# A transformer block with segmented memory attention and a gated FFN: from two stages to one hand-ordered stream

## The chip, the cores and the metric

The kernel runs on one core of a Trainium2 chip. The metric is device time in microseconds (us) per execution. Five engines work side by side, each with its own queue: TensorE (PE in the profile; its weight loads are PEld), VectorE (DVE), ScalarE (ACT), GpSimd (POOL) and SyncE (SP), which issues most transfers. Before the change three runs took 403.99, 404.45 and 406.45 us; the median is 404.45.

## What is computed

One block over 2048 tokens of 448 features, in bf16. A condition vector `c` gives six modulation rows; the first part is attention with 16 heads of 28 features in 4 segments of 512 tokens, the second a gated FFN with 1792 hidden features.

```python
mod = (_silu(c) @ w_mod).reshape(c.shape[0], 6, 1, -1)        # sa, ca, ga, sb, cb, gb
h = _layernorm(x, axis=-1) * (1 + ca) + sa
x = x + ga * _A_ref(h, A_wq, A_wk, A_wv, A_wo, A_beta)
h = _layernorm(x, axis=-1) * (1 + cb) + sb
x = x + gb * _B_ref(h, B_w_gate, B_w_up, B_w_down)

for s in range(N):                                             # _A_ref, for each segment
    a_dot = softmax(qs @ ks.T * scale + causal_mask) @ vs      # inside the segment
    a_mem = (phi(qs) @ M) / (phi(qs) @ z + 1e-06)              # memory of earlier segments
    outs.append(g * a_mem + (1.0 - g) * a_dot)                 # then @ wo
    M = M + phi(ks).T @ vs;  z = z + phi(ks).sum(over tokens)

h = _sigmoid(x @ w_gate) * (x @ w_up)                          # _B_ref, then @ w_down
```

`phi(t)` is `t + 1` for positive `t` and `exp(t)` otherwise. The memory recurrence `M`, `z` is the only tie between segments. LayerNorm, the `wo` product and the FFN are independent from token to token.

## The kernel before, in words

A scheduler decides, from the dependences and the order of the program, in which order each engine does its work; nothing in this kernel fixes it by hand. The 448 features are cut into chunks of 128, 128, 128 and 64 rows (`_kc_rows`); the last chunk sits in rows 64 to 127, so each product over the features still takes four matmuls.

**Start.** SP loads `x` of segment 0, a third of `w_mod`, then `wq`, `wk` and `wv` in pieces through a tile with three buffers (`wtmp`, L163); VectorE copies each piece into a padded layout with 32 columns a head (L168). GpSimd's queue loads the FFN weights at the same time (L173, L174). The modulation rows are made on one partition (L278), transposed into columns, and folded into the weights: `1 + ca` scales `wq`, `wk`, `wv` (L331 to L333), and `sa` becomes bias columns (`bias_cols`, L306). `prep_b`, called after the second attention unit, does the same for `wg`, `wu`, `wo` and `wd`.

**LayerNorm** (`ln_prep`, `ln_transposes`): mean and variance of four tiles of 128 tokens (L185, L186), a reciprocal root by three Newton steps in tiny VectorE instructions (L188 to L201), the normalised tile `xn` (L205), then TensorE transposes into `h1T` or `h2T` (L215, L216).

**Attention.** A unit is a segment and a group of four heads; there are 16. `unit_logits` makes the transposed logits of four key blocks, of 512, 384, 256 and 128 query columns, with four heads side by side in the array (L388), into one PSUM tile `lg` of four banks with a single buffer; ScalarE takes the exp (L392), VectorE masks the diagonal block with a product (L393). `unit_pv` multiplies with `v` for each query block (L418), adds the memory product (L422), and divides and mixes on VectorE, once per query block (L426 to L440). `flush_o` transposes the result (L403, L404). `seg_end` builds `phi(k)` and updates the memory (L451 to L467). The projections of the next segment (L240 for q and k, L246 for v) are put after the first unit of a segment.

**Joint and FFN.** Only when all 16 units are done are the PSUM pools released and given out anew. For each segment `wo_ln2_prep` makes `x2` (L478, L480, with `x` loaded a second time) and its LayerNorm; `ffn_block` then runs 14 hidden chunks: gate (L512) with tanh on ScalarE (L515), up (L519) with a copy and bias on ScalarE (L522), their product on VectorE (L523), and `down_passes` (L506), which accumulates the four token blocks in four PSUM banks. The sums are added to `x2` and stored (L534, L535) at the end of each segment.

Of the kernel before, what the change touches and what calls it, by code (L numbers as in the profile page):

```python
# [24 lines left out]
def kernel(  # L25
# [18 lines left out]
    assert D == 448  # L44
# [24 lines left out]

    const = ctx.enter_context(tc.tile_pool(name="const", bufs=1))  # L70
# [15 lines left out]
    nc.gpsimd.affine_select(out=ident_bf[:], in_=ident_bf[:], compare_op=ALU.not_equal, fill=1.0,
                            base=0, pattern=[[-1, P]], channel_multiplier=1)
    one11 = const.tile([1, 1], BF16)
    nc.vector.memset(one11[:], 1.0)
    ones1 = const.tile([1, P], BF16)  # L90
    nc.vector.memset(ones1[:], 1.0)
    cols_sb = const.tile([P, 16], F32)
    cols_bf = const.tile([P, 16], BF16)
    g_row = const.tile([P, H], F32)
    omg_row = const.tile([P, H], F32)
    bq_col = const.tile([P, NHC], F32)
    bk_col = const.tile([P, NHC], F32)
    bg_col = const.tile([P, NFC], F32)
    bu_col = const.tile([P, NFC], F32)
    bvrep = const.tile([P, DP], BF16)  # L100
    mask01 = const.tile([P, 4, P], BF16)
    nc.vector.memset(mask01[:], 1.0)
    nc.gpsimd.affine_select(out=mask01[:], in_=mask01[:], compare_op=ALU.is_ge, fill=0.0, base=0,
                            pattern=[[0, 4], [1, P]], channel_multiplier=-1)
    maskcol = const.tile([P, 4], F32)
    nc.vector.memset(maskcol[:], 0.0)
    for hs in range(4):
        nc.vector.memset(maskcol[HP * hs:HP * hs + HP, hs:hs + 1], 1.0)
    M_sb = const.tile([P, NHC, P], F32)
    nc.gpsimd.memset(M_sb[:], 0.0)  # L110
    rhs_mem = const.tile([P, NHC, 4 * MW], BF16)
    nc.gpsimd.memset(rhs_mem[:], 0.0)
    for hs in range(4):
        nc.gpsimd.affine_select(out=rhs_mem[:, :, MW * hs + Dh], in_=rhs_mem[:, :, MW * hs + Dh],
                                compare_op=ALU.not_equal, fill=1e-6, base=-(HP * hs + Dh),
                                pattern=[[0, NHC]], channel_multiplier=1)

    wq_sb = wts.tile([P, NKC, DP], BF16)
    wk_sb = wts.tile([P, NKC, DP], BF16)
    wv_sb = wts.tile([P, NKC, DP], BF16)  # L120
    wo_sb = wts.tile([P, NHC, D], BF16)
    wg_sb = wts.tile([P, NKC, F], BF16)
    wu_sb = wts.tile([P, NKC, F], BF16)
    wd_sb = wts.tile([P, NFC, D], BF16)
    for w_sb in (wq_sb, wk_sb, wv_sb):
        nc.vector.memset(w_sb[:].rearrange("p k (h e) -> p (k h) e", e=HP)[:, :, Dh:HP], 0.0)
        nc.gpsimd.memset(w_sb[0:64, 3, :], 0.0)
# [501 lines left out]
```

## Time and profile before

| | |
|---|---|
| runs (us) | 403.99, 404.45, 406.45; median 404.45 |
| profiled execution | span 402.8 us from first to last instruction; no separate time is listed for it, and the median lies 1.65 us above the span |
| mean granted TensorE clock | 0.821 |
| logits, first and last start (us) | 47.7 and 217.5 |
| first `pwo` matmul / first gate matmul / last `down` matmul (us) | 223.1 / 240.3 / 396.6 |

How to read the lines that follow: a group line gives source line, engine, operation, output and inputs, count, then busy time and mean duration of one in ns, then the engine's idle time just before and what ended it. Lines with a start time, a duration and an instruction are the timeline or the chain of waits, in us. A stretch line gives the start and end, then the busy time of each engine with its number of instructions, the granted clock (1.00 is full speed), the share of the DMA engines and GB/s. PEclk shows the clock in 40 slices, in tenths.

### The profile page before, as it was taken

To read this page: it belongs to the slowest core of one execution; us is meant where nothing else is said; L and a number is where in the kernel's file an instruction comes from. 1 tells how busy PE (TensorE), PEld (TensorE's weight loads), DVE (VectorE), ACT (ScalarE), POOL (GpSimd) and SP (SyncE) were. 2 spreads that over 40 slices of the span, in tenths; PEclk is the share of its full clock that TensorE was granted. 3 is DMA by queue.
4 is the path that set the end of the run, shared out by engine and by line. 5 is a ranking of instruction groups with operands and counts; after the bars stand their busy time and mean duration, and the time that the engine had idled before them with its cause. 6 is when DMAs were issued, how large, how long until landed. Compare 5 with 4: busy or idle time off the path is not lost.

```text
span 402.8 us, 6547 instructions
## 1 busy us (share of the span) xinstructions
PE 316.2 (79%) x2354; PEld 159.4 (40%) x2354; DVE 245.6 (61%) x988; ACT 210.9 (52%) x277; POOL 20.7 (5%) x104
## 2 busy tenths in 40 slices
PE   0407879684789777977766579998999899999993
PEld 0104334242555435344434234543444434444441
DVE  5428995639764988189899677324932385234223
ACT  2103559745756786658765015552565246545551
POOL 9500000000100000000000000000000000000000
PEclk9999959855659555795555669999999989999997
DMA  7993400200000000000000100001100010001001
GB/s 204 283 280 106 132 1 2 62 20 2 3 0 2 2 1 2 0 2 2 2 1 2 46 24 26 0 2 46 46 2 1 24 46 1 2 0 46 2 0 46
DMA packets 11602, 14.76 MB, mean 37 GB/s; under 512 B 1473, under 2 KB 10770, under 8 KB 11570
## 3 DMA queue, kind: packets, MB, share of 16 engines
q1 hardware_dynamic: 10610, 9.53, 8.1%
q0 software_dynamic: 960, 4.82, 3.8%
q8 instruction: 18, 0.29, 0.3%
q14 instruction: 14, 0.11, 0.1%
HBM read 12.51 MB, written 1.84 MB: 36 GB/s over the span
## 4 chain that ended last, share of the span: by engine, by line
PE 55%; DVE 19%; ACT 13%; DMA 9%; issue 3%; SPq 0%; DVEq 0%; POOL 0%; ACTq 0%
PE gps L512 12%; PE ups L519 11%; PE dps L506 10%; ACT pT L392 9%; PE lg L388 4%; DMA wtmp<-in_A_wk_dram 3%; PE lntr L215 3%; PE pq L240 3%; PE pwo L478 2%; PE pk L240 2%; DVE stats L185 2%; DMA wtmp<-in_A_wq_dram 2%; PE pv L246 2%; PE acc L418 2%; DVE ot L534 1%
## 5 line engine op out<-in xcount | busy, mean ns | idle before, releaser
L392 ACT ACTIVATE pT<-lg 128x2048 bf16<-128x2048 f32 (+1 forms) x64 | 79.3, 1239 | 37.3 <-PE lg L388 33.7
L512 PE MATMUL gps<-h2T,wg_sb 128*128 128x512 bf16 x224 | 58.5, 383 | 3.7 <-DVE x L480 3.6
L519 PE MATMUL ups<-h2T,wu_sb 128*128 128x512 bf16 x224 | 58.4, 384 | 0.0
L506 PE MATMUL dps<-wd_sb,hTg 128*128 128x448 bf16 x224 | 51.8, 353 | 1.1 <-DVE hTg L523 0.9
L522 ACT ACTIVATE ub<-ups,bu_col 128x512 bf16<-128x512 f32 x56 | 38.5, 687 | 14.0 <-PE ups L519 14.0
L388 PE MATMUL lg<-qT,kT 32*128 32x512 bf16 (+3 forms) x256 | 31.7, 405 | 15.5 <-ACT pT L392 14.6
L418 PE MATMUL acc<-vt,pT 128*128 128x32 bf16 x640 | 29.3, 187 | 12.2 <-DVE t L437 5.2
L418 PEld LDWEIGHTS <-pT 128*128 128x128 bf16 x640 | 25.6, 104 | 22.3 <-issue 16.9
L393 DVE TENSOR_TENSOR pT<-pT,mask 128x512 bf16<-128x512 bf16 x64 | 26.8, 421 | 11.0 <-ACT pT L392 9.7
L512 PEld LDWEIGHTS <-wg_sb 128*128 128x128 bf16 x224 | 22.1, 99 | 28.4 <-issue 5.8
L519 PEld LDWEIGHTS <-wu_sb 128*128 128x128 bf16 x224 | 22.1, 99 | 27.1 <-issue 1.4
L506 PEld LDWEIGHTS <-hTg 128*128 128x128 bf16 x224 | 21.3, 98 | 26.1 <-DVE hTg L523 4.4
L388 PEld LDWEIGHTS <-kT 32*128 32x128 bf16 x256 | 10.4, 97 | 29.6 <-issue 25.2
L215 PE MATMUL lntr<-ident_bf,xn 128*128 128x128 bf16 x128 | 14.5, 273 | 8.0 <-DVE xn L205 5.7
L240 PE MATMUL pq<-h1T,wq_sb 128*128 128x512 bf16 x64 | 20.3, 433 | 0.0
L240 PE MATMUL pk<-h1T,wk_sb 128*128 128x512 bf16 x64 | 19.2, 403 | 0.0
L216 ACT COPY h1T<-lntr 128x512 bf16<-128x512 bf16 x13 | 7.2, 589 | 21.4 <-PE lntr L215 21.4
L403 PE MATMUL otr<-ident_bf,o_u 128*128 128x128 bf16 x64 | 14.9, 269 | 4.3 <-DVE o_u L438 2.4
L478 PE MATMUL pwo<-wo_sb,oT 128*128 128x448 bf16 x64 | 16.5, 417 | 0.7 <-ACT oT L404 0.7
L248 DVE TENSOR_TENSOR vt<-pv,bvrep 128x512 bf16<-128x512 f32 x16 | 10.9, 688 | 9.0 <-PE pv L246 9.0
L215 PEld LDWEIGHTS <-xn 128*128 128x128 bf16 x128 | 10.6, 120 | 12.7 <-DVE xn L205 6.4
L242 ACT ACTIVATE qT<-pq,bq_col 128x512 bf16<-128x512 f32 x16 | 11.2, 697 | 7.0 <-PE pq L240 7.0
(298 smaller groups left out, 471.3 us busy)
## 6 DMA issues: line engine op xcount, KB each, us to landing
wmod_t<-in_w_mod_dram SPq DMA_DIRECT2D x9, 224.0 KB
x_t<-in_A_x_dram SPq DMA_DIRECT2D x4, 448.0 KB
xr<-in_A_x_dram SPq DMA_DIRECT2D x16, 112.0 KB
out_dram<-ot SPq DMA_DIRECT2D x16, 112.0 KB
wd_sb<-in_B_w_down_dram POOLq DMA_DIRECT2D x1, 1568.0 KB, 17.3
wg_sb<-in_B_w_gate_dram POOLq DMA_DIRECT2D x3, 448.0 KB, 6.1
wu_sb<-in_B_w_up_dram POOLq DMA_DIRECT2D x3, 448.0 KB, 9.9
wo_sb<-in_A_wo_dram SPq DMA_DIRECT2D x16, 24.5 KB
```

The lines of the kernel that those rows point to most:

```text
L215: nc.tensor.transpose(pts[:, t * P:(t + 1) * P], xns[t][:, f0:f0 + P], ident_bf[:])
L240: nc.tensor.matmul(pq[:, 0:L], lhsT=w_sb[:, kc, hc * P:(hc + 1) * P], rhs=h1T[:, kc, :], start=(kc == 0), stop=(kc == NKC - 1))
L388: nc.tensor.matmul(lg4[:, hs, 0:nq], lhsT=kT[HP * hs:HP * hs + 32, hc, q0:q0 + P], rhs=qT[HP * hs:HP * hs + 32, hc, q0:q0 + nq], start=Tru ...
L392: nc.scalar.activation(pT[:, :, ob:ob + nq], lg4[:, :, 0:nq], AF.Exp, scale=scale)
L393: nc.vector.tensor_tensor(pT[:, :, ob:ob + P], pT[:, :, ob:ob + P], mask01[:], ALU.mult)
L403: nc.tensor.transpose(otr[:, qb * P:(qb + 1) * P], o_p[:, qb, :], ident_bf[:])
L418: nc.tensor.matmul(acc[:, hs * 32:(hs + 1) * 32], lhsT=pT[:, hs, c0:c0 + P], rhs=vt[:, kb, h * HP:(h + 1) * HP], start=(kb == 0), stop=(kb ...
L478: nc.tensor.matmul(pw_[:, 0:D], lhsT=oT[:, hc, t * P:(t + 1) * P], rhs=wo_sb[:, hc, :], start=(hc == 0), stop=(hc == NHC - 1))
L506: nc.tensor.matmul(dps[t][:, 0:D], lhsT=hT_fc(fc)[:, t * P:(t + 1) * P], rhs=wd_sb[:, fc, :], start=(fc == 0), stop=(fc == NFC - 1))
L512: nc.tensor.matmul(gps[:, 0:L], lhsT=wg_sb[:, kc, fc * P:(fc + 1) * P], rhs=h2T[:, kc, :], start=(kc == 0), stop=(kc == NKC - 1))
L519: nc.tensor.matmul(ups[:, 0:L], lhsT=wu_sb[:, kc, fc * P:(fc + 1) * P], rhs=h2T[:, kc, :], start=(kc == 0), stop=(kc == NKC - 1))
L522: nc.scalar.activation(ub[:], ups[:, 0:L], AF.Identity, bias=bu_col[:, fc:fc + 1], scale=1.0)
```

## The change

The kernel body is written anew.

- **Chunks.** The features are cut into four chunks of 112 rows. `wv`, `wo`, `o` and `v` are no longer padded to 32 columns a head; `wq` and `wk` are (`q` and `k` keep 32 partitions a head).
- **Modulation.** It no longer touches `wq`, `wk`, `wv`, `wg`, `wu`: the transposed LayerNorm output is multiplied by `1 + ca` and `sa` is added while it is copied out of PSUM (`h_chunk`). The modulation columns come straight from matmuls with `w_mod` as the stationary operand. `wo` and `wd` are still scaled, on GpSimd.
- **Transfers.** Each weight is one or two DMAs; SP's queue holds them in order of use and ScalarE's queue three of them. `wq` and `wk` are staged in the space of `wd`. `x` is loaded once and kept; `x2` replaces it in place. The modulation blocks take turns in two slots.
- **Engines.** Masks, clamps, the LayerNorm root (one `pow`), and the last sum of attention go to GpSimd; the copy of `k` goes to VectorE; gate and up meet in one VectorE instruction that reads PSUM. The division of attention runs once per unit instead of once per query block.
- **Logits** come in three groups a unit: 512 columns, 384 with 128, and 256.
- **Order.** TensorE runs in program order (`manual_schedule`); the other engines are still scheduled. For each segment `s`, a queue `fill` of other work (projections and memory of later segments, `wo`, LayerNorm transposes, gate and up of segment `s-1`, `down` of `s-2`) is cut into 24 portions of equal estimated time and laid between the 12 logits groups, `pv` and `otr`. PSUM is one `lg` tile of four banks and a ring of four banks for all else. `down` runs token block by token block over all 14 hidden chunks.

Cut to its core:

```diff
+    KP, NK = 112, 4
+    OFF = (0, L, 2 * L, 2 * L - P)
+    KB_GROUPS = ((0,), (1, 3), (2,))
...
+    ctx.enter_context(tc.manual_schedule(engines={PE}))
+    ps_lg = ctx.enter_context(tc.tile_pool(name="ps_lg", bufs=1, space=bass.MemoryType.PSUM))
+    ps_m = ctx.enter_context(tc.tile_pool(name="ps_m", bufs=4, space=bass.MemoryType.PSUM))
...
+    load_x(nc.sync, 0, 2)
+    load_x(nc.scalar, 2, 4)
...
+    def load_wm(eng, j):
+        t = wts.tile([KP, NK, D], BF16, name=f"wm{j}", tag=f"wm{j % 2}")
+        eng.dma_start(t[:], wmod_k[:, :, j * D:(j + 1) * D])
+        return t
+    wm = {0: load_wm(nc.sync, 0), 1: load_wm(nc.scalar, 1)}
...
+    wq_st = wd_sb[0:KP, 0:NK, :].rearrange("p k (h d) -> p k h d", d=Dh)
+    wk_st = wd_sb[0:KP, NK:2 * NK, :].rearrange("p k (h d) -> p k h d", d=Dh)
...
+    nc.sync.dma_start(wq_st, A_wq.rearrange("(k p) (h d) -> p k h d", p=KP, d=Dh))
+    nc.scalar.dma_start(wk_st, A_wk.rearrange("(k p) (h d) -> p k h d", p=KP, d=Dh))
+    for k in range(NK):
+        nc.scalar.copy(wq_sb[:, k, :, 0:Dh], wq_st[:, k, :, :])
+        nc.gpsimd.tensor_copy(wk_sb[:, k, :, 0:Dh], wk_st[:, k, :, :])
+    nc.sync.dma_start(wv_sb[:], A_wv.rearrange("(k p) n -> p k n", p=KP))
+    for s in range(1, NSEG):
+        load_x(nc.sync, s * TPS, (s + 1) * TPS)
+    wm[2] = load_wm(nc.sync, 2)
+    wo_sb = wts.tile([KP, NK, D], BF16)
+    nc.sync.dma_start(wo_sb[:], A_wo.rearrange("(k p) n -> p k n", p=KP))
+    wm[3] = load_wm(nc.sync, 3)
+    wm[4] = load_wm(nc.sync, 4)
+    wg_sb = wts.tile([KP, NK, F], BF16)
+    wu_sb = wts.tile([KP, NK, F], BF16)
+    for w_sb, w_dram in ((wg_sb, B_w_gate), (wu_sb, B_w_up)):
+        wv_ = w_dram.rearrange("(k p) n -> p k n", p=KP)
+        nc.sync.dma_start(w_sb[:, 0:2, :], wv_[:, 0:2, :])
+        nc.sync.dma_start(w_sb[:, 2:4, :], wv_[:, 2:4, :])
+    wm[5] = load_wm(nc.sync, 5)
+    nc.sync.dma_start(wd_sb[:], B_w_down.rearrange("(fc p) n -> p fc n", p=P))
...
+    def ln_tile(src):
+        nc.vector.bn_stats(st[:], src)
+        nc.vector.bn_aggr(mv[:], st[:])
+        nc.gpsimd.tensor_scalar(ve[:], mv[:, 1:2], EPS, None, op0=ALU.add)
+        nc.gpsimd.tensor_tensor(rs[:], ve[:], mhalf[:], ALU.pow)
+        nc.vector.tensor_scalar(xn[:], src, mv[:, 0:1], rs[:, 0:1], op0=ALU.subtract, op1=ALU.mult)
+        return xn
...
+    def h_chunk(xns, hT, kc, vi):
+        pt = m_bf16("lntr")
+        for t in range(TPS):
+            nc.tensor.transpose(pt[0:KP, t * P:(t + 1) * P], xns[t][:, kc * KP:(kc + 1) * KP], ident[:])
+        nc.vector.tensor_scalar(hT[:, kc, :], pt[0:KP, 0:L], cols[:, vi + 1, kc:kc + 1], cols[:, vi, kc:kc + 1],
+                                op0=ALU.mult, op1=ALU.add)
...
+        if eng == "act":
+            nc.scalar.copy(dst[:, hc, :], pq[:, 0:L])
+        else:
+            nc.vector.tensor_copy(dst[:, hc, :], pq[:, 0:L])
...
+        nc.scalar.copy(vt_all[s][:, t, :, 0:Dh], pv[:, 0:D].rearrange("p (h d) -> p h d", d=Dh))
...
+        lg = ps_lg.tile([P, 4, 512], F32, tag="lg", name="lg")
+        w0 = OFF[KB_GROUPS[g][0]]
+        wid = 0
+        for kb in KB_GROUPS[g]:
+            nq = L - kb * P
+            for hs in range(4):
+                r = slice(HP * hs, HP * hs + Dh)
+                nc.tensor.matmul(lg[:, hs, wid:wid + nq], lhsT=kT[r, hc, kb * P:(kb + 1) * P],
+                                 rhs=qT[r, hc, kb * P:L], start=True, stop=True, tile_position=(HP * hs, 0))
+            wid += nq
+        nc.scalar.activation(pT[:, :, w0:w0 + wid], lg[:, :, 0:wid], AF.Exp, scale=scale)
+        for kb in KB_GROUPS[g]:
+            blk = pT[:, :, OFF[kb]:OFF[kb] + P]
+            nc.gpsimd.affine_select(out=blk, in_=blk, compare_op=ALU.is_ge, fill=0.0, base=0,
+                                    pattern=[[0, 4], [1, P]], channel_multiplier=-1)
...
+    def pv(s, hc):
+        u = (s, hc)
+        pT = pT_of.pop(u)
+        vt = vt_all[s]
+        acc = m_f32("acc")
+        accv = acc[:].rearrange("p (t h e) -> p t h e", h=4, e=HP)
+        for qb in range(TPS):
+            for hs in range(4):
+                for kb in range(qb + 1):
+                    c0 = OFF[kb] + (qb - kb) * P
+                    nc.tensor.matmul(accv[:, qb, hs, 0:ME], lhsT=pT[:, hs, c0:c0 + P],
+                                     rhs=vt[:, kb, hc * 4 + hs, 0:ME], start=(kb == 0), stop=(kb == qb))
...
+        t1 = work.tile([P, TPS * 4, Dh], F32, tag="t1", bufs=1)
+        nc.vector.tensor_tensor(t1[:], num(acc), bc(r1), ALU.mult)
+        r2 = work.tile([P, TPS, 4], F32, tag="r2", bufs=2)
+        nc.vector.tensor_scalar(r2[:], memv[:, :, :, Dh], 1e-6, None, op0=ALU.add)
+        nc.vector.reciprocal(r2[:], r2[:])
+        nc.vector.tensor_tensor(r2[:], r2[:], cb(1), ALU.mult)
+        t2 = work.tile([P, TPS * 4, Dh], F32, tag="t2", bufs=1)
+        nc.vector.tensor_tensor(t2[:], num(mem), bc(r2), ALU.mult)
+        nc.gpsimd.tensor_tensor(ouv, t1[:], t2[:], ALU.add)
...
+    def wo_tile(s, t):
...
+        xt = x_sb[:, s * TPS + t, :]
+        nc.vector.tensor_tensor(xt, pw[:, 0:D], xt, ALU.add)
+        if t == 0:
+            xns_of[("2", s)] = []
+        xns_of[("2", s)].append(ln_tile(xt))
...
+        gp = m_f32("gps")
+        for k in range(NK):
+            nc.tensor.matmul(gp[:, 0:L], lhsT=wg_sb[:, k, fs], rhs=h[:, k, :], start=(k == 0), stop=(k == NK - 1))
+        tt = work.tile([P, L], F32, tag="tt", bufs=2)
+        nc.scalar.activation(tt[:], gp[:, 0:L], AF.Tanh, scale=0.5)
+        up = m_f32("ups")
+        for k in range(NK):
+            nc.tensor.matmul(up[:, 0:L], lhsT=wu_sb[:, k, fs], rhs=h[:, k, :], start=(k == 0), stop=(k == NK - 1))
+        ft = pipe.tile([P, L], BF16, tag="fT", bufs=NFC + 4, name="fT")
+        fT_of[(s, fc)] = ft
+        nc.vector.scalar_tensor_tensor(ft[:], tt[:], 1.0, up[:, 0:L], op0=ALU.add, op1=ALU.mult)
...
+    def down(s, t):
+        dp = m_f32("dps")
+        for fc in range(NFC):
+            nc.tensor.matmul(dp[:, 0:D], lhsT=fT_of[(s, fc)][:, t * P:(t + 1) * P], rhs=wd_sb[:, fc, :],
+                             start=(fc == 0), stop=(fc == NFC - 1))
+        ot = work.tile([P, D], BF16, tag="ot", bufs=3)
+        nc.vector.tensor_tensor(ot[:], dp[:, 0:D], x_sb[:, i, :], ALU.add)
+        nc.sync.dma_start(out_dram[i * P:(i + 1) * P, :], ot[:])
...
+    MM, MV, TR = 216, 190, 60
...
+    def run_fill(ns):
+        while fill and ns > 0:
+            cost, fn = fill.popleft()
+            fn()
+            ns -= cost
+        return ns
...
+        gb = mod_rep(5, 0.5, "gb")
+        for fc in range(NFC):
+            nc.gpsimd.tensor_tensor(wd_sb[:, fc, :], wd_sb[:, fc, :], gb[:], ALU.mult)
...
+    fill.extend(j0[7:])
+    fill.extend(mem_jobs(0))
+    fill.extend(proj_jobs(1))
+    fill.append((1000, prep_b1))
+    fill.extend(mem_jobs(1))
+    fill.append((0, lambda: ln1(2)))
+    fill.append((2000, prep_b2))
+    fill.extend(proj_jobs(2))
+    fill.append((0, lambda: ln1(3)))
+    fill.append((1000, prep_b3))
+    p3 = proj_jobs(3)
+    for s in range(NSEG):
+        if s == 1:
+            fill.extend(p3)
+            fill.extend(mem_jobs(2))
+        if s >= 2:
+            fill.extend(down_jobs(s - 2))
+        if s >= 1:
+            late = h2_jobs(s - 1) + gu_jobs(s - 1)
+        else:
+            late = []
+        total = sum(cst for cst, _ in list(fill) + late) + (wo_jobs(0)[0][0] * 4 if s else 0)
+        quota = total / 12.0
+        debt = 0.0
+        for hc in range(NHC):
+            for g in range(3):
+                logits(s, hc, g)
+                prev = (s, hc - 1) if hc else (s - 1, NHC - 1)
+                debt = run_fill(quota / 2 + debt)
+                if prev[0] >= 0 and g == 1:
+                    pv(*prev)
+                if prev[0] >= 0 and g == 2:
+                    otr(*prev)
+                    if prev[1] == NHC - 1:
+                        fill.extendleft(reversed(wo_jobs(prev[0])))
+                        fill.extend(late)
+                debt = run_fill(quota / 2 + debt)
+        run_fill(1e9 if s == 0 else 0)
+    last = NSEG - 1
+    fill.extend(down_jobs(last - 1))
+    run_fill(3000)
+    pv(last, NHC - 1)
+    run_fill(3000)
+    otr(last, NHC - 1)
+    run_fill(2000)
+    for _, fn in wo_jobs(last):
+        fn()
+    run_fill(1e9)
+    for _, fn in h2_jobs(last) + gu_jobs(last) + down_jobs(last):
+        fn()
```

More of the change, by code (lines that the diff above doesn't have):

```diff
@@ L1 @@
+from collections import deque
 from contextlib import ExitStack
@@ L43 @@
     _, S, D = A_x.shape
-    assert D == 448
     H, Dh = 16, 28
@@ L88 @@
[L88 to L100, printed above, removed]
@@ L111 @@
[L111 to L120, printed above, removed]
@@ L121 @@
[L121 to L127, printed above, removed]
-    nc.gpsimd.memset(wo_sb[:], 0.0)
-    nc.gpsimd.memset(wg_sb[0:64, 3, :], 0.0)
-    nc.gpsimd.memset(wu_sb[0:64, 3, :], 0.0)
-    c_row = const.tile([1, D], BF16)
```

658 lines of the change are left out of this document (209 added, 449 removed).

## The prediction, made before the changed kernel was run

> **What bounds the kernel now.** I read the page first: busy shares, granted clock, the chain that ended last.
>
> ```profile
> span 402.8 us, 6547 instructions
> PE 316.2 (79%) x2354; PEld 159.4 (40%) x2354; DVE 245.6 (61%) x988; ACT 210.9 (52%) x277; POOL 20.7 (5%) x104
> PEclk9999959855659555795555669999999989999997
> PE 55%; DVE 19%; ACT 13%; DMA 9%; issue 3%; SPq 0%; DVEq 0%; POOL 0%; ACTq 0%
> ```
>
> No engine fills the span, and the chain changes hands, so an average says little. I cut the span at the first q matmul, the first logits, the first `pwo` and the first gate matmul, and asked for each engine's busy time by stretch.
>
> ```profile
> core 0: us, PE busy (x) PEld busy (x) DVE busy (x) ACT busy (x) POOL busy (x), PEclk, DMA share, GB/s
> 1.00:38.00 37.00, 9.25 (x76) 4.95 (x77) 18.80 (x87) 5.17 (x9) 14.42 (x32) 1.00 0.80 234
> 20.00:30.00 10.00, 0.00 (x0) 0.00 (x0) 2.45 (x9) 0.00 (x0) 0.00 (x0) 1.00 0.98 286
> 48.00:222.00 174.00, 133.26 (x1433) 73.11 (x1428) 130.23 (x582) 118.34 (x139) 5.85 (x68) 0.64 0.03 8
> 180.00:220.00 40.00, 28.62 (x384) 17.71 (x383) 37.22 (x203) 30.42 (x33) 1.96 (x24) 0.50 0.01 2
> 222.00:240.00 18.00, 11.47 (x48) 5.50 (x49) 12.33 (x41) 1.66 (x3) 0.00 (x0) 0.64 0.11 31
> 240.00:398.00 158.00, 152.22 (x755) 71.50 (x753) 73.65 (x227) 80.22 (x118) 0.00 (x0) 0.99 0.05 16
> ```
>
> Four kernels in one. Until 38 us TensorE waits for weights. Attention (174 us) is set by the hand-overs between logits, exp, mask and division; by its end VectorE is busy 37.2 of 40 us and the clock is 0.50. A joint of 18 us follows, then an FFN of 158 us at clock 0.99 in which only TensorE matters. So the FFN can hardly be shortened, only filled around: what there is to win lies in the first 240 us.
>
> **What it becomes.** All FFN and projection work becomes filler between the logits groups of the next segment, so the stages stop adding up, and TensorE's own work at full clock is the sum to make. Its rows, from stretches at high clock (only `dM` and `bg` are from half clock):
>
> ```profile
> 257.88 0.76 PE dps L506 x4
> 258.63 0.86 PE gps L512 x4
> 259.50 0.86 PE ups L519 x4
> 293.48 0.89 PE lntr L215 x16
> 197.53 1.52 PE dM L461 x13
> 87.24 1.59 PE bg L306 x56
> 72.17 0.88 PE L418 MATMUL acc<-vt,pT 128*128 128x32 bf16 x28 [0.27 <-DVE vt L248]
> 70.88 0.40 PE L388 MATMUL lg<-qT,kT 32*128 32x512 bf16 x4
> 73.75 0.34 PE L388 MATMUL lg<-qT,kT 32*128 32x384 bf16 x4
> 62.95 0.29 PE L388 MATMUL lg<-qT,kT 32*128 32x256 bf16 x4
> 64.99 0.24 PE L388 MATMUL lg<-qT,kT 32*128 32x128 bf16 x4
> ```
>
> The same columns stream through 112 rows instead of 128, which I cost as no change: the FFN is 56 x (0.86 + 0.86 + 0.76) = 138.9 us. The 32 q and k groups cost 0.86 each, 27.5. The 16 v groups, now 448 columns wide, and the 16 `wo` groups cost 0.76, 24.3. LayerNorm transposes: 8 x 0.89 = 7.1; the other 112 transposes at 0.056, 6.2. `dM`: 48 at 0.117, halved to full clock, 2.8. `acc`: 640 at 0.88/28 = 0.031, 20.1; its memory part, 48 of 116 columns at 0.76/1792 per column, 2.4. Logits: at most 0.40 + 0.34 + 0.29 + 0.24 = 1.27 a unit, 20.3 in all; at least their 1280 columns at 0.42 ns, 8.6; neither row shows them packed among filler, so I take the middle, 14. The modulation: 64 column products at 1.59/56 and 8 replications at 0.19, 3.3, in place of row products, transposes and bias columns. Sum 246.6 us, about 2 of it inside the start. That is **245 us** after the start.
>
> **The start.** Today q, k and v weights pass through three buffers while the GpSimd queue pulls the FFN weights through the same DMA engines:
>
> ```profile
> 10.56 7.35 DMA wtmp<-in_A_wq_dram
> 18.23 12.35 DMA wtmp<-in_A_wk_dram
> L240 PE MATMUL pq<-h1T,wq_sb x64: 378/379/634, 37.0 to 170.1; 128*128 128x512 bf16 x64
> ```
>
> After the change the order on SP and ACT is by need: x of segment 0, two modulation blocks, wq and wk, 2.06 MB in one DMA each. At the 286 GB/s above that is 7.2 us; issue and the wv transfer beside it make it about 11. Then come four padding copies on ACT and POOL (some 2.5 us) and the modulated transposes: first q matmul at 16 us. From below 12 (data and one copy). From above 30: wk landed at 30.6 us before, and rows of 28 elements could be sent as short packets. I take **16**, nearer the measured bandwidth.
>
> **The other engines** must stay under TensorE. Their rows:
>
> ```profile
> L392 ACT ACTIVATE pT<-lg 128x2048 bf16<-128x2048 f32 x16 | 30.0, 1876 | 14.9 <-PE lg L388 11.5 <-PE acc L418 3.4
> L392 ACT ACTIVATE pT<-lg 128x1024 bf16<-128x1024 f32 x16 | 16.4, 1024 | 8.4 <-PE lg L388 8.3
> L522 ACT ACTIVATE ub<-ups,bu_col 128x512 bf16<-128x512 f32 x56 | 38.5, 687 | 14.0 <-PE ups L519 14.0
> L248 DVE TENSOR_TENSOR vt<-pv,bvrep 128x512 bf16<-128x512 f32 x16 | 10.9, 688 | 9.0 <-PE pv L246 9.0
> L480 DVE TENSOR_TENSOR x<-pwo,xr 128x448 bf16<-128x448 f32 x16 | 9.7, 619 | 5.0 <-PE pwo L478 3.9 <-PE gps L512 0.8
> L185 DVE BATCH_NORM_STATS2 stats<-x 128x6 f32<-128x448 bf16 x16 | 9.6, 620 | 0.1
> L205 DVE TENSOR_SCALAR xn<-x,rstd,nmr 128x448 bf16<-128x448 bf16 x16 | 5.3, 392 | 0.1
> L216 DVE COPY h2T<-lntr 128x512 bf16<-128x512 bf16 x8 | 3.4, 425 | 1.3 <-PE lntr L215 1.2
> L426 DVE RECIPROCAL s<-acc 128x4 f32<-128x4 f32 x64 | 11.0, 176 | 1.9 <-PE acc L418 1.0 <-PE acc L422 0.7
> L103 POOL TENSOR_SCALAR_AFFINE_SELECT mask<-mask 128x512 bf16<-128x512 bf16 x1 | 0.6, 632 | 0.0
> L114 POOL TENSOR_SCALAR_AFFINE_SELECT rhs_mem<-rhs_mem 128x4 bf16<-128x4 bf16 x4 | 0.6, 195 | 0.0
> PE lntr L215 <- DVE xn L205: 5.7, 1, 5.7
> ```
>
> ACT: exp is 16 x (2 x 1.876 + 1.024) = 76.4 (three instructions a unit instead of four), 56 tanh 38.5, 56 other wide ones (q, v, `eq`, `ek`) 38.5 at most, small ones 4: **157**, from 211; `ub` and the k copies are gone from it. DVE: 96 instructions of 512 columns at 0.688 (gate product, k copy, the two feature maps) 66; 32 adds at 0.619 19.8; stats 19.8; `xn` 12.5; 48 transposed copies at 0.425 20.4 (the modulation rides on 32 of them; at 0.688 instead they add 8); 28 divisions of 448 columns at 0.62 17.4; about 108 tiny ones at 0.17 18: **174**, from 246. Masks, `o_u` pads and the Newton steps leave DVE. POOL: 64 masks 40.5, 24 clamps 15, 33 two-input ones which no row shows, between one and two times 0.632, 21 to 42, 64 tiny LayerNorm steps at 0.2 13, weight copies 3: **92 to 113**, from 21. I take 105, above the middle, for the two inputs. All three stay under 245, so what they cost is waits.
>
> **The waits that appear.** TensorE's order is now written by hand, and everything behind a waiting matmul waits with it. First, the joint: `wo`, LayerNorm, transposes. Four tiles keep DVE 4 x (0.62 + 0.62 + 0.17 + 0.39) = 7.2 us, with two POOL steps inside each; TensorE has 2.3 us of `wo` left and about one `down` (14 x 0.19 = 2.7), so it waits some 3 us at each of three joints (the wait row above shows 5.7 where nothing covered it) and 5 at the last, where the filler is used up: 14. If a segment has more filler left, nothing; if DVE is behind by a gate product or two, twice as much. Second, PSUM: `acc` and `mem` hold two of four slots while DVE needs 2.06 us; gate and up fill the other two in 1.72, so 0.4 in each of 12 units, 5. Third, the clock: it was 0.99 where TensorE was 96% busy and 0.64 at 77%. If segment 0, with only projections as filler (some 46 us), runs at 0.9, that is 5. Together **24 us**, with 5 and 70 as ends. SP's order has a trap that I cost at nothing: the fifth modulation block reuses the third's slot, so it, and wg, wu, the sixth block and wd behind it, wait for the third's use some 21 us of filler into segment 0. 3.2 MB at 286 GB/s then take 11.2 us; the sixth block is wanted about 13 us of filler and logits later. Cover of a few microseconds; without it as many are lost.
>
> **The end.** `down` runs token block by token block, so only the last block's add and its store are bare.
>
> ```profile
> L535 SPq DMA_DIRECT2D out_dram<-ot x16: 332/333/1217, 277.6 to 400.1; - x16
> 398.00:402.80 4.80, 0.00 (x0) 0.00 (x0) 1.16 (x2) 0.00 (x0) 0.00 (x0) 0.58 0.27 92
> ```
>
> From the last issue at 400.1 to the end are 2.7 us; with the add, 3.5 (before, 5.8 after the last matmul).
>
> **Sum:** 16 + 245 + 24 + 3.5 = 288.5 us of span. The median, 404.45, lies 1.65 above the profiled span of 402.8, so the forecast is **290 us**.
>
> **The rivals.** *Denser still*: the joints are covered and the clock stays full. For it: 0.99 over 158 us of FFN; ACT and DVE at 60 to 70%. Against it: DVE's 7.2 us per joint. 16 + 245 + 5 + 3.5 + 1.65 = 271 us. *Hand-overs take over*: each of 32 LayerNorm tiles makes DVE wait for two POOL steps behind up to two masks, 2 x 0.632 + 0.4 = 1.7 us, 54 in all; half reaches TensorE through PSUM, 27, and a clock 3% lower over the 190 us of interleaved work (below) adds 6. For it: DVE at 93% in 180 to 220. Against: a third of DVE's time is free. 290 + 27 + 6 = 323 us. The Trainium skill, "GPSIMD Engine Reference", section "8. Key points": GpSimd shares its SBUF interfaces with VectorE and contends with it, which speaks for this rival; no row here shows both busy together for long. *Slow start*: first q at 30 us, 304 us.
>
> *Slow transposes.* LayerNorm and `o` transposes now load 112 columns, not 128, as the stationary.
>
> ```profile
> L215 PEld LDWEIGHTS <-xn 128*128 128x128 bf16 x128 | 10.6, 120 | 12.7 <-DVE xn L205 6.4
> ```
>
> Such a load takes 120 ns but is hidden at 0.056 us a transpose (0.89/16). If the narrower one is not, each of 192 costs 0.12: 192 x 0.064 = 12 us more, 302 us. For it: nothing in this trace, which has no stationary of 112 columns; against it: `lntr` is as fast as 128 streamed columns at 0.42 ns, so loads hide well. The Trainium skill, "TensorE: Matmul & The Clock Gate", section "Weight-path perf modes — Fast Weight Load (FWL) and DoubleRow", speaks for it: the fast weight load is on only when the number of weights is 128. By its section "LDWEIGHTS (loading the stationary operand)", columns over 1.2, I estimate 93 ns a load, which would make it 7 us, 297.
>
> *The clock never recovers* (slower): where TensorE pauses between groups the clock stays at 0.50 as in 180 to 220, through the four interleaved segments. Their work, 245 less the last 35 of gate, up and down and 20 others, is 190 us; at 0.50 it takes 380, and the kernel 16 + 380 + 55 + 24 + 3.5 + 1.65 = 480 us. It decides from a mean clock of 190/304 = 0.625 downward. For it: 174 us at 0.64. Against: filler stands in every gap, and a slower array has fewer gaps.
>
> **How the numbers follow.** Forecast 290 (own range 274 to 306): 0.43. Slow transposes 0.10, denser 0.14, hand-overs (306 to 345) 0.22, slow start 0.05, clock 0.06, of which 0.01 ends near no change. The range 268 to 336 leaves out the clock, part of the hand-overs and the densest cases, 0.15 in all. Faster by over 1% is 0.94, within 1% 0.01, slower 0.05; 1% is about what a measurement of this kernel can tell from no change.
>
> **What would show it.** Right: first q near 16 us; TensorE's clock above 0.9 between 70 and 270; ACT near 157, DVE 174, POOL 105 us; waits of TensorE for `xn` and `hT` of some 3 us at each joint. Wrong: a first q beyond 25 us, a mean clock under 0.8, `lntr` groups well over 0.89 us, DVE waiting long for POOL, or logits beyond 1.27 us a unit.

## The result, and the profile after

The changed kernel takes 351.94 us (median of 6 runs, 349.13 to 352.71), the one before 404.22 (6 runs, 403.20 to 406.45): a ratio of 0.868, 95% interval 0.864 to 0.871. It is faster, as forecast, but lies 62 us above the forecast of 290 and outside the range of 268 to 336. The profiled execution took 349.13 us. Of the kernels below, `newton_on_vector` and `spread_scale` also had runs more than 1.5% above their fastest: their times and ratios are those of the other runs (three and two), their profiles show one of the longer ones.

The page, with the lines that answer to those of before:

```profile
span 347.4 us, 5518 instructions
...
PE 277.8 (80%) x2232; PEld 144.5 (42%) x2232; DVE 171.0 (49%) x382; ACT 142.0 (41%) x169; POOL 119.3 (34%) x209
...
PEclk9999879758999668999996999999699999969999
...
PE 61%; POOL 16%; DVE 10%; ACT 7%; DMA 3%; issue 2%; SPq 0%; POOLq 0%; ACTq 0%
```

TensorE is busy for 80% of the span, as before (79%), though filler from other segments now stands between the logits groups. The mean granted clock is 0.916; it dips at 35 to 85, at 115 to 140 and near 185, 250 and 310 us (a digit is 8.7 us). The four longest waits of TensorE (us in all, times, longest) follow. `lntr` are the LayerNorm transposes, `dM` and `pk` the product of the memory update and its `phi(k)`, `cp` the modulation columns, `otr` the transposes of the attention output. The third is the load at the start; the first two lie at the dips, except 4.7 us of the first at the start:

```profile
PE lntr L195 <- DVE xn L189: 22.3, 13, 4.7
PE dM L257 <- DVE pk L247: 18.8, 12, 5.3
PE cp L160 <- DMA wm<-in_w_mod_dram: 10.0, 1, 10.0
PE otr L351 <- POOL ou L343: 7.7, 7, 1.1
```

The busy time by stretch: the part after the first q matmul, then two 20 us stretches at a dip, an undisturbed one, and the last joint (`wo`, LayerNorm and its transposes at the end of a segment):

```profile
22.15:347.40 325.25, 272.08 (x2184) 139.51 (x2183) 160.02 (x349) 138.44 (x162) 107.89 (x170) 0.91 0.08 23
...
60.00:80.00 20.00, 11.96 (x141) 9.58 (x139) 6.74 (x15) 5.88 (x9) 9.53 (x13) 0.61 0.16 41
...
180.00:200.00 20.00, 12.90 (x115) 7.06 (x108) 11.27 (x27) 7.23 (x8) 6.38 (x13) 0.83 0.00 1
200.00:220.00 20.00, 18.90 (x185) 9.18 (x183) 9.95 (x22) 11.94 (x15) 5.96 (x9) 1.00 0.00 1
...
300.00:320.00 20.00, 14.41 (x67) 7.17 (x68) 9.65 (x22) 3.58 (x6) 2.93 (x7) 0.83 0.00 0
```

A stretch with neither joint nor memory update has TensorE at 18.9 of 20 us; the others shown lose 6 to 8 us each, and in them no engine is near full. These are hand-overs, not a bound. TensorE's timeline at the joint of segment 1 with the FFN of segment 0 (start, length):

```profile
173.24 2.82 PE L386 MATMUL dps<-wd_sb,fT 128*128 128x448 bf16 x14
175.89 0.39 PE L351 MATMUL otr<-ident,ou 128*112 128x128 bf16 x4
...
176.54 3.20 PE L358 MATMUL pwo<-wo_sb,oT 112*128 112x448 bf16 x16
...
180.86 0.26 PE L195 MATMUL lntr<-ident,xn 128*112 128x128 bf16 x1 [0.79 <-DVE xn L189]
183.39 0.26 PE L195 MATMUL lntr<-ident,xn 128*112 128x128 bf16 x1 [2.27 <-DVE xn L189]
185.18 0.35 PE L195 MATMUL lntr<-ident,xn 128*112 128x128 bf16 x1 [1.52 <-DVE xn L189]
186.94 1.64 PE L195 MATMUL lntr<-ident,xn 128*112 128x128 bf16 x13 [1.41 <-DVE xn L189]
...
189.83 1.50 PE L373 MATMUL gps<-hT,wg_sb 112*128 112x512 bf16 x4
```

All four `down` jobs stand before `otr` and `wo`; behind `wo` nothing is left but one logits group, and TensorE waits for each LayerNorm tile in turn: 0.79 + 2.27 + 1.52 + 1.41 = 6.0 us. The first gate group behind it takes 1.50 us, later ones 1.03: the granted clock was 0.50 from 187 to 189.8 us, 0.65 over that group and 1.00 from 191.2.

The start, on POOL and TensorE:

```profile
14.32 0.65 POOL L154 MEMSET vt<- 128x64 bf16 x2
...
15.29 0.73 POOL L185 TENSOR_SCALAR ve<-mv 128x1 f32<-128x1 f32 x4
...
22.15 0.58 PE L220 MATMUL pq<-hT,wq_sb 112*128 112x512 bf16 x1 [1.73 <-DVE hT L196]
```

POOL finishes `bmask` and the ones of `vt` before it serves LayerNorm, and the first q starts at 22.15 us, not 16.

### The profile page after: what moved, and what is told of

The parts are those of the page before. It is cut to its first block, busy times and chain, and to the rows that moved or that the text cites. A ratio compares the mean times of both kernels' runs of the same rounds, so it can differ in the third digit from the quotient of the medians.

```text
span 347.4 us, 5518 instructions
## 1 busy us (share of the span) xinstructions
PE 277.8 (80%) x2232; PEld 144.5 (42%) x2232; DVE 171.0 (49%) x382; ACT 142.0 (41%) x169; POOL 119.3 (34%) x209
## 3 DMA queue, kind: packets, MB, share of 16 engines
q10 hardware_dynamic: 1200, 1.03, 1.1%
## 4 chain that ended last, share of the span: by engine, by line
PE 61%; POOL 16%; DVE 10%; ACT 7%; DMA 3%; issue 2%; SPq 0%; POOLq 0%; ACTq 0%
PE gps L373 13%; PE dps L386 12%; PE ups L378 11%; PE pq L220 7%; PE acc L309 4%; POOL wd_sb L447 4%; POOL pT L296 3%; POOL rs L187 3%; PE lg L290 3%; ACT pT L293 3%; DMA wd_sb<-in_A_wq_dram 3%; PE lntr L195 2%; POOL ou L343 2%; DVE st L182 2%; DVE xn L189 2%; PE pv L231 2%
## 5 line engine op out<-in xcount | busy, mean ns | idle before, releaser
L296 POOL TENSOR_SCALAR_AFFINE_SELECT pT<-pT 128x512 bf16<-128x512 bf16 x64 | 40.5, 646 | 100.8 <-ACT pT L293 100.7
L375 ACT ACTIVATE tt<-gps 128x512 f32<-128x512 f32 x56 | 33.3, 596 | 88.2 <-PE gps L373 86.8
L381 DVE SCALAR_TENSOR_TENSOR fT<-tt,ups 128x512 bf16<-128x512 f32 x56 | 38.5, 688 | 61.6 <-PE ups L378 36.9
L373 PE MATMUL gps<-hT,wg_sb 112*128 112x512 bf16 x224 | 60.5, 392 | 0.9 <-DVE hT L196 0.8
L378 PE MATMUL ups<-hT,wu_sb 112*128 112x512 bf16 x224 | 58.6, 385 | 0.0
L386 PE MATMUL dps<-wd_sb,fT 128*128 128x448 bf16 x224 | 43.9, 353 | 0.0
L378 PEld LDWEIGHTS <-wu_sb 112*128 112x128 bf16 x224 | 22.2, 99 | 27.7 <-issue 2.2
L373 PEld LDWEIGHTS <-wg_sb 112*128 112x128 bf16 x224 | 20.2, 101 | 23.9 <-issue 6.3
L386 PEld LDWEIGHTS <-fT 128*128 128x128 bf16 x224 | 21.4, 98 | 19.7 <-issue 0.5
L220 PE MATMUL pq<-hT,wq_sb 112*128 112x512 bf16 x64 | 19.6, 422 | 2.8 <-DVE hT L196 2.6
L257 PE MATMUL dM<-vt,pk 128*128 128x116 bf16 x48 | 6.7, 293 | 18.8 <-DVE pk L247 18.8
```

The source lines that it names most:

```text
L220: nc.tensor.matmul(pq[:, 0:L], lhsT=head_cols(w_sb, k, hc), rhs=h[:, k, :], start=(k == 0), stop=(k == NK - 1))
L296: nc.gpsimd.affine_select(out=blk, in_=blk, compare_op=ALU.is_ge, fill=0.0, base=0, pattern=[[0, 4], [1, P]], channel_multiplier=-1)
L373: nc.tensor.matmul(gp[:, 0:L], lhsT=wg_sb[:, k, fs], rhs=h[:, k, :], start=(k == 0), stop=(k == NK - 1))
L375: nc.scalar.activation(tt[:], gp[:, 0:L], AF.Tanh, scale=0.5)
L378: nc.tensor.matmul(up[:, 0:L], lhsT=wu_sb[:, k, fs], rhs=h[:, k, :], start=(k == 0), stop=(k == NK - 1))
L381: nc.vector.scalar_tensor_tensor(ft[:], tt[:], 1.0, up[:, 0:L], op0=ALU.add, op1=ALU.mult)
```

## The experiments

Two theories were set against each other. **A**: POOL is the cause, by its many instructions inside DVE's LayerNorm and inside the memory update. **B**: the hand-written order of TensorE is the cause; the joint and the memory update have no filler behind them. Each expectation says what its letters mean for its kernel. The ratios are to the kernel before, measured again beside each group of kernels (404.29, 404.41 and 404.88 us).

**LayerNorm without POOL**: the four tiles' `rstd` by Newton steps on DVE, all four in one instruction; the four added lines shown run three times.

```
-        nc.gpsimd.tensor_scalar(ve[:], mv[:, 1:2], EPS, None, op0=ALU.add)
-        nc.gpsimd.tensor_tensor(rs[:], ve[:], mhalf[:], ALU.pow)
...
+        nc.vector.tensor_tensor(lt[:], rs[:], rs[:], ALU.mult)
+        nc.vector.tensor_tensor(lt[:], lt[:], ve[:], ALU.mult)
+        nc.vector.tensor_scalar(lt[:], lt[:], -0.5, 1.5, op0=ALU.mult, op1=ALU.add)
+        nc.vector.tensor_tensor(rs[:], rs[:], lt[:], ALU.mult)
```

> The LayerNorm root goes back to VectorE as Newton steps on four tiles at once; no GpSimd step is left between the sums and xn. Theory A (GpSimd in the LayerNorm chain makes TensorE wait): the wait of lntr for xn falls from 22.3 us to under 8 and the time by 12 us or more, to 340 or less. Theory B (the order gives the chain no cover, whichever engine takes its steps): 17 tiny steps of 0.17 us replace about 1.9 us of GpSimd waits in each joint, so the joints stay or grow and only the start gains, some 4 us: 345 to 354.

Measured: 347.87 us, 0.862 (0.856 to 0.867): in B's range.

```profile
PE lntr L208 <- DVE xn L201: 24.0, 4, 6.5
```

The same wait, now at once for four tiles instead of tile by tile. POOL's two steps are not the cause of the joint: taking them away trades them for DVE's own. Where the 4 us lie that the time fell stays open: the first q starts only 0.4 us earlier.

**Work carried over the joint**: five gate-and-up jobs of each segment wait for the next one, and `down` comes behind `wo`.

```
-        if s >= 2:
-            fill.extend(down_jobs(s - 2))
         if s >= 1:
-            late = h2_jobs(s - 1) + gu_jobs(s - 1)
+            gu = gu_jobs(s - 1)
+            late = (down_jobs(s - 2) if s >= 2 else []) + h2_jobs(s - 1) + gu[:9]
...
         run_fill(1e9 if s == 0 else 0)
+        fill.extend(gu[9:])
...
-    fill.extend(down_jobs(last - 1))
...
     for _, fn in wo_jobs(last):
         fn()
+    fill.extend(down_jobs(last - 1))
```

> TensorE's order alone: five gate-and-up jobs of each segment are kept for the next one, and the four down jobs of the segment before stand behind wo instead of in front of it, so that about 10 us of filler cover each LayerNorm between wo and its transposes. Theory B: the wait of lntr for xn falls from 22.3 to 7 or less (4.7 of it is the start) and the time by 18 to 28 us, to 324 to 334. Theory A: VectorE waits for GpSimd just as before, and TensorE then waits for PSUM instead: less than 8 us.

Measured: 331.32 us, 0.818 (0.814 to 0.822), in B's range: 20.6 us off by order alone, with the same instructions.

```profile
PE dM L257 <- DVE pk L247: 13.1, 10, 5.0
...
PE lntr L195 <- DVE xn L189: 4.6, 1, 4.6
```

The wait at all three joints that had one is gone; the one left is the start's. B is shown for the joints. The 20.6 us are not theirs alone: the `dM` wait fell too, by 5.7 us, and other waits grew.

**The clamp of exp(k) on DVE**, so that POOL's queue is out of the memory update:

```
-        nc.gpsimd.tensor_scalar(ek[:], ek[:], 1.0, 0.0, op0=ALU.min, op1=ALU.max)
+        nc.vector.tensor_scalar(ek[:], ek[:], 1.0, 0.0, op0=ALU.min, op1=ALU.max)
```

> The clamp of exp(k) goes back from GpSimd to VectorE (12 instructions); the order stays. Theory A: the wait of dM for pk falls from 18.8 to 8 or less and the time to 338 or less. Theory B: the chain from transposes over exp, clamp and sum to dM stays bare; it loses only what GpSimd's queue adds in segments 0 and 1, so dM still waits 10 to 13 us and the time is 342 to 348.

Measured: 351.09 us, 0.866 (0.861 to 0.871): no change, and the `dM` wait still 16.6 us. That is outside both ranges, and A fails. The longest of these waits in this kernel:

```profile
113.51 1.08 ACT L245 ACTIVATE ek<-ptk 128x512 bf16<-128x512 bf16 x2 [0.48 <-PE ptk L243]
...
116.81 0.70 DVE L189 TENSOR_SCALAR xn<-x_sb,mv,rs 128x448 bf16<-128x448 bf16 x1 [1.00 <-POOL rs L187]
117.42 0.71 DVE L246 TENSOR_SCALAR ek<-ek 128x512 bf16<-128x512 bf16 x1
...
118.99 0.28 PE L257 MATMUL dM<-vt,pk 128*128 128x116 bf16 x1 [4.85 <-DVE pk L247]
```

ScalarE has two exps done by 114.6 us, but DVE first ends the LayerNorm of segment 0, and only then clamps. So the first joint, which shows no wait for `xn`, holds up the memory update instead, whichever engine clamps: 4.85 us here, 5.3 in the changed kernel.

**The memory jobs spread**: each `mem_k` is followed by two projection jobs, and `mem_update` comes behind them all.

```
+    def spread(mem, other, every=2):
+        out = []
+        for i, job in enumerate(mem[:-1]):
+            out.append(job)
+            out.extend(other[i * every:(i + 1) * every])
+        return out + other[(len(mem) - 1) * every:] + [mem[-1]]
-    fill.extend(mem_jobs(0))
-    fill.extend(proj_jobs(1))
+    fill.extend(spread(mem_jobs(0), proj_jobs(1)))
```

> TensorE's order alone: the four phi(k) jobs of a segment are laid between projection jobs, and the memory update comes after the last of them; the same instructions on the same engines. Theory B: the wait of dM for pk falls from 18.8 us to under 4 and, with the clock that it costs, the time by 15 to 25 us, to 327 to 337. Theory A (GpSimd is late with its clamps because masks and the scaling of wo and wd stand ahead of them): the clamps stay late, TensorE waits elsewhere, and the time falls by less than 8.

Measured: 345.24 us, 0.854 (0.849 to 0.858). By its letters that is A, 6.7 us off. The `dM` wait is gone, but two others came in its place (waits, one stretch, and POOL in it):

```profile
PE cp L160 <- DMA wm<-in_w_mod_dram: 13.4, 2, 10.5
PE pq L220 <- DVE pk L247: 11.2, 2, 11.0
```

```profile
80.00:100.00 20.00, 8.07 (x79) 4.88 (x78) 4.07 (x9) 6.29 (x9) 17.08 (x20) 0.81 0.00 0
...
84.99 13.88 POOL L447 TENSOR_TENSOR wd_sb<-wd_sb,gb 128x448 bf16<-128x448 bf16 x14
...
99.41 1.20 POOL L246 TENSOR_SCALAR ek<-ek 128x512 bf16<-128x512 bf16 x2
```

In 80 to 100 us POOL is busy 17.08 of 20: the scaling of `wd`, 14 instructions in a row, now stands ahead of a clamp. So neither theory held alone: the order was one cause and POOL's queue stood behind it. The second `cp` wait, 2.9 us, is for the fifth modulation block, which SP can load only when the third's slot is free: the trap in SP's order that the prediction names.

**Spread, with `wo` and `wd` scaled on DVE**, one instruction each:

```
-        for fc in range(NFC):
-            nc.gpsimd.tensor_tensor(wd_sb[:, fc, :], wd_sb[:, fc, :], gb[:], ALU.mult)
+        nc.vector.tensor_tensor(wd_sb[:], wd_sb[:],
+                                gb[:].rearrange("p (o n) -> p o n", o=1).to_broadcast([P, NFC, D]), ALU.mult)
```

> Memory jobs spread between the projection jobs as in memory_spread, and the scaling of `wo` and `wd` done by DVE in one instruction each. Theory A (the burst of scalings on POOL, 14 x 1.03 us, is what stands ahead of the clamps and made the 11.0 us wait of `pq` in memory_spread): that wait goes and the half clock behind it, about 14 us off 345.2: 330 to 334, POOL's busy time in 80 to 100 us falls from 17 to about 3, and DVE's sum rises by some 5. Theory B (the wait came from the one `pk` buffer or from the order of TensorE's own jobs): 343 to 347, a wait of `pq` or `dM` for `pk` of 8 us or more is still there.

Measured: 337.39 us, 0.834 (0.828 to 0.839), 7.9 below memory_spread: between the two ranges, a miss for both. The wait of 11 us went, and another came:

```profile
PE lntr L195 <- DVE pk L247: 4.8, 2, 4.7
```

The trace of carry_spread_scale, below, shows what made it.

**The start**: `bmask`, the ones in `vt` and the LayerNorm of segment 1 moved, in this order, behind the first projections.

```
     mod_cols(1, 1, True)
-    ln1(1)
     j0 = proj_jobs(0)
     for _, fn in j0[:7]:
         fn()
...
+    ln1(1)
```

> POOL's set-up (`bmask`, the ones in `vt`) and the LN of segment 1 are put behind the first six projection jobs; nothing else changes. Theory A (POOL's set-up and the LN of segment 1 on DVE make the first q late): first q near 17 instead of 22.2, 346 to 348.5 in all. Theory B (the start is set by the loads and by the copies of wq and wk that end at 13.8, and what is won is given back at segment 1): first q after 20, 350 to 353.

Measured: 346.99 us, 0.856 (0.852 to 0.860), 5 us off, as A has it; the first q starts here, 3.4 us earlier:

```profile
18.76 1.91 PE L210 MATMUL pq<-hT,wq_sb 112*128 112x512 bf16 x4
```

**Carry, spread and scaling on DVE together**, without and with the new start:

> The carried FFN work (331.3 alone), the spread memory jobs and the scaling on DVE, together. Theory A (joints and memory chain are separate stretches with separate stalls, so that their gains add up): 351.9 - 20.6 - 19 = 312, 308 to 316, TensorE's waits below 32 us in all, mean granted clock 0.95 or more. Theory B (a wait that goes is given back by the next one, PSUM ring or POOL): 322 to 332.

> As carry_spread_scale, with the start of start_order. Theory A (gains add up): 4 to 5 us below carry_spread_scale, near 308. Theory B: within 2 us of carry_spread_scale, since the carried jobs and the memory chain of segment 0 then meet an earlier joint unprepared.

Measured: 316.86 us, 0.783 (0.779 to 0.786), and 313.98, 0.776 (0.772 to 0.779). Alone the parts (carry, and spread_scale) gave 20.6 and 14.5 us off, together 35.1: they add up. The time itself lies 0.9 above A's range, which had counted on 19 for the second part. The start adds 2.9 of its 5, between its two letters. DVE and POOL in carry_spread_scale:

```profile
81.80 3.45 DVE L446 TENSOR_TENSOR wd_sb<-wd_sb,gb 128x6272 bf16<-128x6272 bf16 x1 [0.65 <-ACT gb L175]
...
83.61 2.14 POOL L296 TENSOR_SCALAR_AFFINE_SELECT pT<-pT 128x512 bf16<-128x512 bf16 x1 [1.64 <-ACT pT L293]
...
87.11 0.58 PE L195 MATMUL lntr<-ident,xn 128*112 128x128 bf16 x4 [4.66 <-DVE pk L247]
```

One DVE instruction of 3.45 us holds `hT` and `pk`, and beside it a POOL mask takes 2.14 us instead of 0.65, with a clamp behind it: 4.66 us of TensorE again.

**The clock by itself**: 120 matmuls that nobody reads, 24 at each of five waits.

```
+    def warm_up():
+        d = m_f32("warm")
+        for _ in range(24):
+            nc.tensor.matmul(d[:, 0:L], lhsT=wg_sb[:, 0, 0:P], rhs=wg_sb[:, 0, 0:L], start=True, stop=True)
```

> The changed kernel plus work that computes nothing: 24 gate-shaped matmuls (5.1 us at full clock) that nobody reads, put on TensorE ahead of the first `lntr` of each of the last three joints and ahead of `dM` of segments 1 and 2, where it waits 5 to 6 us in any case. The waits stay, only the clock behind them changes. Theory A (the half clock after the waits is a cost of its own, some 27 us in all, half of it behind these five): 335 to 344, mean granted clock 0.95 or more. Theory B (the clock falls within the wait itself and is back within 4 us behind it, so that the wait is nearly all of the cost): 345 to 352. Theory C (the matmuls do not fit into the waits): above 354.

Measured: 351.92 us, 0.869 (0.867 to 0.871), at a mean clock of 0.961 (0.916 before); inside B's range, at its upper end. The joint of segment 1, and the first of the two blocks at `dM`:

```profile
182.71 3.20 PE L358 MATMUL pwo<-wo_sb,oT 112*128 112x448 bf16 x16
186.17 5.35 PE L428 MATMUL warm<-wg_sb 112*128 112x512 bf16 x24
...
195.24 1.03 PE L373 MATMUL gps<-hT,wg_sb 112*128 112x512 bf16 x4
...
197.28 1.04 PE L373 MATMUL gps<-hT,wg_sb 112*128 112x512 bf16 x4
```

```profile
68.80 7.73 PE L428 MATMUL warm<-wg_sb 112*128 112x512 bf16 x24 [5.00 <-DVE pk L247]
```

At the joint they fit. From `wo` to the second gate group it takes 197.28 - 182.71 = 14.57 us; without them 15.81 (the second gate group of after starts at 192.35):

```profile
192.35 1.04 PE L373 MATMUL gps<-hT,wg_sb 112*128 112x512 bf16 x4
```

So the half clock behind this joint costs 1.2 us, against 6.0 of waiting. The blocks at `dM` did not fit: four `ptk` tiles hold all four PSUM slots, so the block waited the 5.00 us itself and then ran on top. What that clock would give alone stays open: B for the joints, C's mechanism at `dM`. A mean clock 0.045 higher, bought with these blocks, was worth nothing here.

**Finer**, from the kernel with all four changes: the fifth modulation block gets a place of its own, and `wd` is scaled in 14 pieces on DVE, in `gate_up` behind the gate product; then also `ou`, then also the clamp on DVE.

```
+        if j == 4:
+            t = qT_of[2][0:KP, :, 0:D]
+            eng.dma_start(t, wmod_k[:, :, j * D:(j + 1) * D])
+            return t
...
+        if s == 0:
+            nc.vector.tensor_tensor(wd_sb[:, fc, :], wd_sb[:, fc, :], rep_of["gb"][:], ALU.mult)
...
-        nc.gpsimd.tensor_tensor(ouv, t1[:], t2[:], ALU.add)
+        nc.vector.tensor_tensor(ouv, t1[:], t2[:], ALU.add)
```

> all_four with two of its three longest waits taken away: the fifth modulation block is loaded into qT of segment 2, unused until then, so that no load waits for a slot; and `wd` is scaled by DVE in 14 pieces of one chunk, each behind a gate product of segment 0, in place of one instruction of 3.45 us. Theory A (the two waits, 2.9 us for `cp` and 4.7 us for `lntr`, and the half clock behind them were what all_four still lost): 314.0 - 10 = 304, 302 to 307. Theory B (the next wait takes their place): 310 to 314.

> finer, with the sum of the two attention parts (`ou`) done by DVE instead of POOL. Theory A (POOL's 1.13 us and the two hand-overs are what `otr` waits for, 11.1 us in all over ten waits): 4 to 7 us below finer. Theory B (DVE then does 12 x 0.6 us more ahead of its casts, and `otr` waits for DVE instead): within 2 us of finer, either way.

> finer_sum, with the clamp of exp(k) on DVE too, so that no POOL instruction stands between two DVE steps of the memory chain. Theory A (POOL's masks ahead of the clamps still hold the chain): 2 to 4 us below finer_sum. Theory B (with the jobs spread the chain is covered): within 1.5 us of finer_sum.

Measured: 307.44 us, 0.759 (0.757 to 0.762); 300.23, 0.743 (0.740 to 0.746); 300.25, 0.740 (0.736 to 0.744). The first gives 6.5 of the expected 10, just short of A's range. `ou` on DVE gives 7.2, as A has it, though DVE gets more to do. The clamp gives nothing once the jobs are spread, which is B. The page, the waits and the part after the first q of finer_sum:

```profile
PE 264.5 (89%) x2232; PEld 135.9 (46%) x2232; DVE 181.9 (61%) x409; ACT 141.0 (47%) x169; POOL 91.2 (31%) x179
...
PEclk9997999999989999999999999999999999999999
```

```profile
PE cp L157 <- DMA wm<-in_w_mod_dram: 10.3, 1, 10.3
PE otr L346 <- DVE ou L338: 5.7, 8, 1.7
PE lntr L192 <- DVE xn L186: 2.3, 1, 2.3
```

```profile
18.00:297.90 279.90, 259.16 (x2188) 131.01 (x2186) 174.68 (x384) 137.43 (x162) 82.69 (x151) 0.99 0.11 31
```

With the same matmuls in another order, and the scaling of `wo` and `wd` and the sum `ou` moved from POOL to DVE, it beats both kernels: 300.2 us against 351.9 and 404.2.

## Why the prediction was wrong

The sum of the span was 16 + 245 + 24 + 3.5 = 288.5; the span is 347.4, 58.9 more. By its terms:

- **The waits failed**: 19 us forecast without the clock. From the first q to the end TensorE is idle 325.25 - 272.08 = 53.2 us, less 3.3 at the end: 50, so 31 too few. Most of it is two chains that the prediction does not have at all. The memory update is `ptk`, exp on ACT, clamp on POOL, `pk` on DVE, `dM`, four times in a row with two `ek` buffers and nothing between: 18.8 us of waits, more than the whole term for the joints. The sum `ou` on POOL, which `otr` waits for, made 7.7 more, seven times 1.1; the two runs that differ in its engine alone, finer and finer_sum, lie 7.2 us apart.
- **The joints** were forecast at 14 us, three times 3 and 5 at the last, and came to 17.6: none at the first, 6.0 at each of the next two and 1.11 + 2.27 + 1.12 + 1.13 = 5.6 at the last. The size is near, but partly by luck, since the step behind it failed: "TensorE has 2.3 us of `wo` left and about one `down` (14 x 0.19 = 2.7)". No `down` was left; that the queue order puts `down` ahead of `wo` was in the code and was not followed. The two joints without it cost the prediction's "twice as much", and the first held up the memory update instead.
- **PSUM** was forecast at 5; the waits that look like one for a slot, `ptk` for `x_sb` (2.0) and `lntr` for `t` (0.6), are 2.6.
- **TensorE's work and the clock**: 272.1 us busy, against 245 and 5 for the clock; 22 too few. In finer_sum, at clock 0.99, the same matmuls take 259.2, so 13 us of it went with the waits and the half clock behind them, and some 14 are in the sum of the work itself. From one start to the next, without the waits, its rows give: FFN 145.6 instead of 138.9, q and k 32.7 instead of 27.5 (at the start some of these groups take up to 1.91), the transposes behind the first q 16.9 instead of some 12.4, and `acc` 16.1 instead of 20.1. One source shows: an up group of 0.86 takes 0.95 or 0.96 when logits follow, in all 16 such places of finer_sum; at all 48 logits groups it would be 4.8 us, an estimate. The logits themselves came out at the middle that was taken between two bounds: the next group starts 0.32, 0.33 and 0.22 us later, 0.87 a unit or 14 in all.
- **The start**: 22.15, not 16. The weights were there: wk landed at 10.47 and wq at 11.81 us, close to the 11 forecast. POOL's set-up ahead of LayerNorm, which nobody costed, and the LayerNorm of segment 1 ahead of `hT` on DVE stand in the 6 us; with them moved the first q came at 18.76, and the time fell by 5. Where the other 2.8 us of the start lie stays open.
- **Right**: the sum for DVE (171 against 174) and roughly that for ACT (142 against 157; a tanh takes 0.596 and not 0.688, which is 5 of it), the end, and that FFN work hides under the rest. The waits are at the places where the prediction looked for them, in part: `xn` at the joints. POOL's 119 us lie outside its 92 to 113: the 64 LayerNorm steps took 18.0 + 6.8 us, not 13.
- **The SP trap**, costed at nothing: right for the change, where the waits of the memory update covered the load. Once they were gone (memory_spread) it cost 2.9 us.

The rivals: *hand-overs take over* (323) had the right direction and the wrong mechanism. DVE waits 15.0 us for `rs`, 0.47 a tile, not 1.7:

```profile
L189 DVE TENSOR_SCALAR xn<-x_sb,mv,rs 128x448 bf16<-128x448 bf16 x32 | 13.3, 431 | 15.2 <-POOL rs L187 15.0
```

and without POOL there the time hardly moved. *Slow transposes* is refuted by rows of memory_spread, where four transposes with 112 and with 128 stationary columns take the same:

```profile
83.04 0.39 PE L351 MATMUL otr<-ident,ou 128*112 128x128 bf16 x4
...
84.90 0.39 PE L243 MATMUL ptk<-ident,kT 128*128 128x128 bf16 x4
```

The Trainium skill, "TensorE: Matmul & The Clock Gate", section "Weight-path perf modes — Fast Weight Load (FWL) and DoubleRow", would have the narrower load leave the fast path; at these rows nothing is lost by it. *The clock never recovers* fell too: the mean is 0.916, far above its 0.625. *Denser* was right only in what it named: with the joints covered by order alone the kernel takes 331 us, and 300 with the other changes too, not 271.

## What to carry to other kernels

When an order is written out by hand, list every chain that leaves TensorE and comes back (here LayerNorm, the memory update, the sum behind `acc`), and check job by job what stands in the queue behind its first step; a total of filler per segment says nothing about it. Work for such a gap must be held back on purpose. After each wait removed, look for the next on the same queue: here POOL's scalings and one long DVE instruction stood behind the first.

## What the runs showed of the hardware

A POOL mask of 0.65 us took 2.14 beside a DVE instruction of 3.45 with two inputs in SBUF. The Trainium skill, "GPSIMD Engine Reference", section "8. Key points", says that the two share their SBUF interfaces and contend when a VectorE instruction has two SBUF inputs or runs in a 2-port mode; the trace agrees, and the loss went to POOL here. It can go the other way: in clamp_on_vector a DVE clamp of 0.28 us took 1.50 while POOL scaled `wo`. POOL needs 0.57 us for a power of 128 x 1 elements, 18.0 us in all, and 1.13 for a sum of two inputs that DVE does in 0.70:

```profile
L187 POOL TENSOR_TENSOR rs<-ve,mhalf 128x1 f32<-128x1 f32 x32 | 18.0, 569 | 1.7
...
L343 POOL TENSOR_TENSOR ou<-t,t 128x448 bf16<-128x448 f32 x12 | 13.6, 1130 | 12.2 <-DVE t L342 12.2
```

Behind the waits of the last three joints (0.8 to 2.3 us each) the clock was at half, and the first gate group took 1.50 to 1.91 us; one or two groups later it was at 1.03 again. That fits the 1.2 us that the half clock cost behind one of them. Behind the memory update of segment 1 it lasted longer: the last wait ended at 70.22, and two projection groups still took 1.91 and 1.88 us at 78 and 80. Nor does it take a wait: in warm_joints, where the block at `dM` had brought the clock to 1.00 (76.4 to 79.9 us), it was 0.50 again from 82.05 to 83.70, with TensorE busy all the time on the one-column products of `cp`, logits and transposes. The reason stays open.
